# Gated attention with two MoE layers on one core: a shorter weight decode, two tiles in three terms, one chunk's decay a unit ahead, two chunks' outputs in two units

## The chip, the cores and the metric

The kernel runs on one core of one Trainium2 chip. The metric is device time in microseconds (us), the median of several executions of the same program; lower is better. The engines are TensorE (PE, matmuls; its weight loads are listed as PEld), VectorE (DVE), ScalarE (ACT), GpSimd (POOL) and SyncE (SP), whose queue issues nearly all DMAs. Each engine works through its own instructions strictly in program order and waits on semaphores of the others.

## The reference

What is computed, cut to its core (B=4, H=8, S=768, D=48; 3072 tokens, d_model 384, d_ff 2048):

```python
f = 1.0 / (1.0 + np.exp(-f_logit))
for t in range(S):
    state = f[:, :, t, :, None] * state + np.einsum('bhd,bhe->bhde', k[:, :, t], v[:, :, t])
    y[:, :, t] = np.einsum('bhd,bhde->bhe', q[:, :, t], state)
x = y.transpose(0, 2, 1, 3).reshape(B * S, H * D)
h = np.maximum(x @ w_in, 0.0)
x = h * h @ w_out                                      # MoE layer 0
h = x @ w_in2
x = np.where(h > 0, h, np.exp(np.minimum(h, 0)) - 1) @ w_out2   # MoE layer 1
```

The weights reach the chip as 64-bit floats. The kernel decodes them to 32-bit floats itself.

## The kernel before

**Units.** The 3072 tokens are six blocks of 512, and each layer has 16 tiles of 128 hidden columns. A unit u is one pair of block and tile. In unit u the kernel issues `up` of unit u (PE: the hidden values `ph`) and then `down` of unit u-2 (PE: the outputs `y`); `between` on ACT and DVE makes the operands `gg`, `gh`, `gl` of `down` from `ph`. Units 0 to 15 are block 0 of layer 0, units 16 to 31 block 1, and so on; units from 96 on are layer 1.

**Three terms and one term.** A value is split into a high and a low part (`hi`, `lo`, type fp32r), and a product is high x high + low x high + high x low, three matmuls of fp32r. In block 0 the tiles below `WHOLE` do it another way in `down`: one matmul in full f32 with the weights as decoded, which a DMA (`store_weights`, L411 and L413, on SP) copies into the weight tile; the second half of such a tile is split later, in block 1 (`split_rest`). Tiles from `WHOLE` on are split whole in block 0 (`split_up`, L434 on ACT for the high part and L435 on DVE for the low one).

**Decode.** In block 0 the decode of a weight tile is `begin` (two ACT instructions, L71 and L73) and, one unit later, `finish` (two DVE instructions, L81 and L82). L73 turns the top byte of a double's low word into its three highest bits and writes them as a 32-bit word over that low word; `finish` shifts, merges the three bits, and merges the sign. Layer 1 uses `decode`, which is not touched; it holds a DVE shift of the same shape (L59).

**Attention.** The sequence is 24 chunks g of 128 tokens (four batches x six). Chunks 0 to 3 and the first decodes are issued in START, an order written out by hand as a string of letters (f: load the forget logits `ff`; g: gate; d: decay scan on DVE; U: `up`; and so on). The later chunks are planned: `NEAR[g]` = a gives the unit in which chunk g meets its keys, and the other steps of the chunk stand at fixed distances from it. With d = a - 4 (g up to 12): load `ff` at d-2, load q and k and gate at d, decay at d+1, scale at d+2, load v at d+1. Steps planned for unit 1 or earlier are dropped by `at`; START has them. `f5` stands in START, and for chunk 5 (a = 8, d = 4) the plan loads `ff` once more in unit 2. The outputs of a chunk are `a_far` (PE L293, which adds the state, then a small ACT copy `seen`, L300), `a_out` (PE L308, ACT L316), `a_rows` (six small DMAs, L324) and `a_hi`, `a_lo` (the chunk's part of the block's `xh` and `xl`). For most chunks another chunk's `a_near` lies between `a_far` and `a_out` in the same unit; chunks 7 and 23, the last of their blocks, have none there. `plan` is issued ahead of a unit's matmuls, `behind` after them.

Of the kernel before, what the change touches and what calls it, by code (L numbers as in the profile page):

```python
# [11 lines left out]
F32 = mybir.dt.float32  # L12
F32R = mybir.dt.float32r
I32 = mybir.dt.int32
U32 = mybir.dt.uint32
U8 = mybir.dt.uint8
I64 = mybir.dt.int64
AF = mybir.ActivationFunctionType
ALU = mybir.AluOpType
PSUM = bass.MemoryType.PSUM  # L20

B, H, S, D = 4, 8, 768, 48
# [15 lines left out]
STAGED = 27  # L38
DIRECT = 3
EARLY = 14  # L40
WHOLE = 10
NEAR = dict(zip(range(B, NG), (5, 8, 10, 12, 19, 21, 23, 25, *range(28, 4 * NG - 23, 4))))
ORDER = np.r_[64:128, 63:-1:-1]
DMIN = 2.0**-52
# [21 lines left out]
def begin(nc, raw, out):  # L66

    words = raw.bitcast(U32).rearrange("p (n two) -> p n two", two=2)
    top = raw.bitcast(U8).rearrange("p (n b) -> p n b", b=8)[:, :, 3]
    hi, lo = words[:, :, 1], words[:, :, 0]  # L70
    nc.scalar.activation(out.bitcast(F32), hi.bitcast(F32), AF.Copy, scale=2.0**-112)  # L71

    nc.scalar.activation(lo, top, AF.Copy, scale=1 / 32, bias=-31 / 64)  # L73


def finish(nc, raw, out):

    words = raw.bitcast(U32).rearrange("p (n two) -> p n two", two=2)
    hi, lo = words[:, :, 1], words[:, :, 0]
    V = nc.vector  # L80
    V.scalar_tensor_tensor(out=out, in0=out, scalar=3, in1=lo, op0=ALU.logical_shift_left, op1=ALU.bitwise_or)  # L81
    V.scalar_tensor_tensor(out=out, in0=hi, scalar=0x80000000, in1=out, op0=ALU.bitwise_and, op1=ALU.bitwise_or)  # L82


def chunked(ctx, tc, ff, qk, vk, vz, wraw, mask, ident, flag, out):
# [6 lines left out]
    nc = tc.nc  # L92
    V, A, G, PE = nc.vector, nc.scalar, nc.gpsimd, nc.tensor

    one = ctx.enter_context(tc.tile_pool(name="one", bufs=1))
    two = ctx.enter_context(tc.tile_pool(name="two", bufs=2))
# [31 lines left out]
    def load_f(g):  # L128
        if g in (2, 3):
            if g == 2:  # L130
                st["f23"] = wpool.tile([ROWS, 2, 521], F32, tag="w", name="f23")
            t = st["f23"][:, g - 2]
        else:
            t = two.tile([ROWS, 521], F32, tag="ff", name=f"ff{g}")
        nc.sync.dma_start(out=t, in_=ff[g])
        st.setdefault(g, {})["ff"] = t

    def load_qk(g):
# [251 lines left out]
    def begin_weights(f):  # L390

        if f < EARLY:
            if f % 2 == 0:
                st["pair"] = wpool.tile([128, 2, 2 * DM], U32, tag="w", name=f"pair{f}")
            b = st["pair"][:, f % 2]
        else:
            b = two.tile([128, 2 * DM], U32, tag="dec", name=f"dec0_{f}")
        begin(nc, raws[0, f], b)
        decs[f] = b

    def finish_weights(f):
        finish(nc, raws.pop((0, f)), decs[f])

    def store_weights(f):

        wt[0, f] = t = wpool.tile([128, 2, 2, DM], F32R, tag="w", name=f"w0_{f}")
        if f >= WHOLE:
            return
# [6 lines left out]
    def split_up(f):  # L415
        b = decs.pop(f).bitcast(F32)
        if f < WHOLE:
            split(wt[0, f][:, :, 0:1], b[:, :DM])
# [13 lines left out]
    def split(t, b):  # L432
        hi, lo = (t[:, a].rearrange("r i m -> r (i m)") for a in range(2))
        A.activation(hi, b, AF.Copy)  # L434
        V.tensor_tensor(out=lo, in0=b, in1=hi, op=ALU.subtract)  # L435
# [11 lines left out]
    n1 = sum(layer == 0 for layer, _, _ in BLOCKS)  # L447
# [4 lines left out]
    def pieces(i, f):  # L452

        n = BLOCKS[i][2]
        return (slice(0, n // 2), slice(n // 2, n)) if (i, f) == final else (slice(0, n),)
# [21 lines left out]
    def between(i, f):  # L477
        layer, t0, n = BLOCKS[i]
        if i == 0 and f < WHOLE:

            r = one.tile([128, n], F32, tag="r", name=f"r{i}_{f}")
            gg = three.tile([128, n], F32, tag="gh", name=f"gg{i}_{f}")
            A.activation(r, hs[i, f][0], AF.Relu)
            A.activation(gg, r, AF.Square)
            hs[i, f] = (None, None, gg)
            return
        gh = three.tile([128, n], F32R, tag="gh", name=f"gh{i}_{f}")
        gl = three.tile([128, n], F32R, tag="gl", name=f"gl{i}_{f}")
        r = one.tile([128, n], F32, tag="r", name=f"r{i}_{f}")
        gg = two.tile([128, n], F32, tag="gg", name=f"gg{i}_{f}")  # L490
        if layer:
            t = two.tile([128, n], F32, tag="ff", name=f"t{i}_{f}")
        for c, ph in zip(pieces(i, f), hs[i, f]):
            if layer == 0:
                A.activation(r[:, c], ph, AF.Relu)  # L495
                A.activation(gg[:, c], r[:, c], AF.Square)

                if i == n1 - 1 or (i == 0 and f >= EARLY):
                    A.activation(gh[:, c], r[:, c], AF.Square)
                else:  # L500
                    V.tensor_tensor(out=gh[:, c], in0=r[:, c], in1=r[:, c], op=ALU.mult)  # L501
            else:
                A.activation(r[:, c], ph, AF.Relu, scale=-1.0)  # L503

                A.activation(t[:, c], r[:, c], AF.Tanh, scale=-0.5)  # L505
                A.activation(r[:, c], r[:, c], AF.Exp, scale=-1.0)  # L506
                V.scalar_tensor_tensor(out=t[:, c], in0=r[:, c], scalar=1.0, in1=t[:, c], op0=ALU.add, op1=ALU.mult)  # L507
                V.scalar_tensor_tensor(out=gg[:, c], in0=ph, scalar=0.0, in1=t[:, c], op0=ALU.max, op1=ALU.add)  # L508
                if (i, f) == final:
                    A.activation(gh[:, c], gg[:, c], AF.Copy)  # L510
                else:
                    V.tensor_copy(gh[:, c], gg[:, c])

            if (i, f) == final or i == 0:
                V.tensor_tensor(out=gl[:, c], in0=gg[:, c], in1=gh[:, c], op=ALU.subtract)
        hs[i, f] = (gh, gl, gg)
# [40 lines left out]
    plan, behind = {}, {}  # L557

    def at(slot, f, *args, to=plan):

        if slot > 1:
            to.setdefault(slot, []).append((f, args))
# [2 lines left out]
        at(f - 5, load_raw, 0, f)  # L565
    for g in range(B, NG):
        a = NEAR[g]
        d = a - (4 if g <= 3 * B else 6)
        at(d - 2, load_f, g)
        at(d, load_qk, g)  # L570
        at(d, a_gate, g)
        at(d + 1, a_decay, g)
        at(d + 2, a_scale, g)
        for h in (a_keys, a_transposed):
            at(a - (1 if g <= 3 * B else 2), h, g)
        at(d + 1 if g < B + 2 else max(d + 1, NEAR[g - 1] + 1), load_v, g)
        over = g > B and g != 2 * B
        if over:
            at(a, a_far, g - 1)
        at(a, a_near, g)  # L580
        if over:
            at(a, a_out, g - 1)
            at(a + 1, a_rows, g - 1)
        at(a, a_mask, g)
        at(a, a_states, g)
        if g in (2 * B - 1, NG - 1):
            for h in (a_far, a_out):
                at(a + 1, h, g)
            at(a + 2, a_rows, g)
            for h in (a_hi, a_lo):  # L590
                at(a + 3, h, g, to=behind)
        else:
            for h in (a_hi, a_lo):
                at(NEAR[g + 1] + 3, h, g)
# [6 lines left out]
    for f in range(NF):  # L601
        at(max(f - 3, 2 if f > 3 else 0), begin_weights, f)
        at(f - 2, finish_weights, f)
        if f < WHOLE:
            at(f + (NF - 2 if f < DIRECT else NF), split_rest, f)
# [10 lines left out]
    with tc.manual_schedule():  # L616
# [13 lines left out]
        for _ in range(3):  # L630
# [3 lines left out]
            "M": lambda: nc.sync.dma_start(out=msk, in_=mask),  # L634
            "T": lambda: [nc.sync.dma_start(out=tri[c:c + 64], in_=mask[c:c + 64, 64 - c:128 - c]) for c in (0, 64)],
            "f": load_f, "q": load_qk, "v": load_v, "r": lambda f: load_raw(0, f),
            "g": a_gate, "d": a_decay, "c": a_scale, "s": a_scores, "t": a_transposed, "m": a_mask, "k": a_state,
            "y": a_direct, "h": a_hi, "l": a_lo,
            "x": a_whole, "b": begin_weights, "w": finish_weights, "C": store_weights, "S": split_up, "W": busy,
            "U": lambda f: up(0, f), "B": lambda f: between(0, f),  # L640
            "L": lambda f: low(0, f),
        }
# [110 lines left out]
@with_exitstack  # L753
def gated_attention_moe(ctx: ExitStack, tc: tile.TileContext, ff, qk, vk, vz, nat, wraw, mask, ident, out):
    pool = ctx.enter_context(tc.tile_pool(name="flag", bufs=1))
    flag = pool.tile([1, 1], I32, name="flag")
    with ExitStack() as inner:
        chunked(inner, tc, ff, qk, vk, vz, wraw, mask, ident, flag, out)
    rv = tc.nc.values_load(flag[0:1, 0:1], min_val=0, max_val=1)
    with tc.If(rv == 1):  # L760
        with ExitStack() as inner:
            general(inner, tc, nat, wraw, ident, out)
# [58 lines left out]
```

## Time and profile before

| what | value |
|---|---|
| median of 3 runs | 885.45 us (886.34, 885.35, 885.45) |
| the profiled execution | 884.29 us |
| its span, first to last instruction | 882.2 us |
| PE busy | 867.3 us (98%) |
| DVE, ACT, POOL busy | 556.1, 454.2, 277.8 us |
| granted TensorE clock over the span | 0.998 |

The span is the part of the execution that the trace covers; 2.1 us of the profiled execution lie outside it. Matmuls are pipelined and their ends are modelled, so a busy PE can still be waiting: what counts is the distance from the start of one matmul to the start of the next. The profiled execution is 1.16 us shorter than the median of the three runs.

### The profile page before, as it was taken

What the parts mean: (1) busy time and instruction counts of PE and PEld (TensorE: products, weight loads), DVE (VectorE), ACT (ScalarE), POOL (GpSimd) and SP (SyncE); (2) the same over time, 40 slices, a digit from 0 to 9 for tenths busy, and PEclk for the clock granted to TensorE, in tenths of its full rate; (3) what the DMA queues carried; (4) which work ended last, traced back from release to release, by engine and by line L of the source; (5) the groups of instructions that cost most, each with busy time, mean ns of one, the idle gap of its engine ahead of it and who ended that gap; (6) DMA issues with size and microseconds to landing.
All of it is one profiled execution on the core that took longest, in us unless ns stands there. A gap on an engine that the chain in (4) does not pass through costs nothing.

```text
span 882.2 us, 16003 instructions
## 1 busy us (share of the span) xinstructions
PE 867.3 (98%) x6262; PEld 701.4 (80%) x6262; DVE 556.1 (63%) x841; ACT 454.2 (51%) x812; POOL 277.8 (31%) x248
## 2 busy tenths in 40 slices
PE   7999999999999999999999999999999999999996
PEld 4666788888888888888888888888888888888885
DVE  8989797876778777744331655655654664664543
ACT  5868745555445555454554544544444444444443
POOL 2011065423333333323232323233232332322331
PEclk9999999999999999999999999999999999999999
DMA  9993222235434434422676300100200100100001
GB/s 291 343 306 125 78 88 86 89 111 183 155 119 151 151 117 158 143 77 107 249 277 225 131 13 1 62 10 4 69 1 18 55 1 34 38 1 37 1 1 39
DMA packets 35779, 91.46 MB, mean 104 GB/s; under 512 B 5728, under 2 KB 12128, under 8 KB 35696
## 3 DMA queue, kind: packets, MB, share of 16 engines
q1 hardware_dynamic: 35552, 90.24, 30.6%
q8 instruction: 50, 0.82, 0.4%
q14 instruction: 33, 0.27, 0.1%
q10 hardware_dynamic: 144, 0.13, 0.0%
HBM read 64.78 MB, written 22.02 MB: 98 GB/s over the span
## 4 chain that ended last, share of the span: by engine, by line
PE 92%; DMA 4%; DVE 1%; SPq 1%; issue 0%; ACT 0%; DVEq 0%
PE y L538 44%; PE ph L474 44%; DMA raw<-wraw 2%; DMA q<-qk 1%; PE o L293 1%; PE o L308 1%; PE tp L209 1%; PE sk_a L232 1%; PE sk_a L241 1%; PE sk_h L241 0%; DVE ds L181 0%; PE sk_h L232 0%; DVE xl L355 0%; DVE pair L82 0%; DVE pair L81 0%
## 5 line engine op out<-in xcount | busy, mean ns | idle before, releaser
L521 POOL TENSOR_TENSOR gl<-gg,gh 128x512 fp32r<-128x512 f32 x175 | 234.2, 1338 | 451.8 <-PE ph L474 192.1
L538 PE MATMUL y<-gh,wf 128*128 128x512 f32 (+1 forms) x582 | 177.7, 387 | 0.0
L507 DVE SCALAR_TENSOR_TENSOR t<-r,t 128x512 f32<-128x512 f32 (+1 forms) x97 | 71.4, 736 | 154.8 <-ACT r L506 154.6
L538 PE MATMUL y<-gh,w 128*128 128x512 f32 x516 | 158.9, 389 | 0.0
L503 ACT ACTIVATE r<-ph 128x512 f32<-128x512 f32 (+1 forms) x97 | 57.8, 596 | 181.4 <-PE ph L474 176.5
L474 PE MATMUL ph<-xh,w 128*128 128x512 f32 x558 | 148.0, 400 | 0.3 <-DVE w L435 0.3
L474 PE MATMUL ph<-xh,wf 128*128 128x512 f32 (+1 forms) x582 | 146.4, 387 | 0.0
L538 PEld LDWEIGHTS y<-gh,wf 128*128 128x128 f32 x582 | 108.8, 188 | 22.2
L474 PEld LDWEIGHTS ph<-xh,wf 128*128 128x128 f32 x582 | 108.6, 188 | 22.3
L474 PEld LDWEIGHTS ph<-xh,w 128*128 128x128 f32 x558 | 101.4, 188 | 22.6 <-DVE w L435 0.9
L538 PEld LDWEIGHTS y<-gh,w 128*128 128x128 f32 x516 | 96.8, 188 | 20.2
L538 PE MATMUL y<-gl,wf 128*128 128x512 f32 (+1 forms) x291 | 112.5, 387 | 0.0
L495 ACT ACTIVATE r<-ph 128x512 f32<-128x512 f32 x86 | 51.3, 596 | 106.6 <-PE ph L474 89.2
L538 PE MATMUL y<-gl,w 128*128 128x512 f32 x258 | 100.4, 389 | 0.0
L474 PE MATMUL ph<-xl,wf 128*128 128x512 f32 (+1 forms) x291 | 81.0, 387 | 0.0
L474 PE MATMUL ph<-xl,w 128*128 128x512 f32 x279 | 78.5, 390 | 0.0
L501 DVE TENSOR_TENSOR gh<-r 128x512 fp32r<-128x512 f32 x68 | 46.8, 689 | 43.0 <-ACT r L495 43.0
L508 DVE SCALAR_TENSOR_TENSOR gg<-ph,t 128x512 f32<-128x512 f32 (+1 forms) x97 | 66.6, 686 | 10.4 <-DVE t L507 0.5
L538 PEld LDWEIGHTS y<-gl,wf 128*128 128x128 f32 x291 | 54.6, 188 | 11.2
L474 PEld LDWEIGHTS ph<-xl,wf 128*128 128x128 f32 x291 | 54.4, 188 | 11.1
L505 ACT ACTIVATE t<-r 128x512 f32<-128x512 f32 (+1 forms) x97 | 61.0, 629 | 3.1
L506 ACT ACTIVATE r<-r 128x512 f32<-128x512 f32 (+1 forms) x97 | 61.0, 628 | 3.1
(112 smaller groups left out, 1026.6 us busy)
## 6 DMA issues: line engine op xcount, KB each, us to landing
raw<-wraw SPq DMA_DIRECT2D x32, 768.0 KB, 7.1
wst<-w SPq DMA_DIRECT2D x16, 768.0 KB, 3.3
wf<-wst SPq DMA_DIRECT2D x16, 768.0 KB, 4.7
ff<-ff SPq DMA_DIRECT2D x23, 227.9 KB, 7.0
k<-qk SPq DMA_DIRECT2D x22, 224.0 KB, 3.4
q<-qk SPq DMA_DIRECT2D x22, 224.0 KB, 4.4
x2d<-yo SPq DMA_DIRECT2D x18, 256.0 KB, 2.8
x<-x2d SPq DMA_DIRECT2D x18, 256.0 KB, 3.2
```

The source lines that it names most:

```text
L209: PE.transpose(tp[:, p, 0:ROWS], k[:, p], idt[:ROWS, :ROWS])
L232: PE.matmul(sc[j][64 * c:64 * c + 64, p], k[lo:hi, p, 64 * c:64 * c + 64], q[lo:hi, p, 64 - 64 * c:128 - 64 * c], start=True, stop=True,)
L474: PE.matmul(ph, w[:, a, 0, 128 * k:128 * k + 128], b[:, k, c], start=(m == 0), stop=(m == len(todo) - 1))
L495: A.activation(r[:, c], ph, AF.Relu)
L501: V.tensor_tensor(out=gh[:, c], in0=r[:, c], in1=r[:, c], op=ALU.mult)
L503: A.activation(r[:, c], ph, AF.Relu, scale=-1.0)
L505: A.activation(t[:, c], r[:, c], AF.Tanh, scale=-0.5)
L506: A.activation(r[:, c], r[:, c], AF.Exp, scale=-1.0)
L507: V.scalar_tensor_tensor(out=t[:, c], in0=r[:, c], scalar=1.0, in1=t[:, c], op0=ALU.add, op1=ALU.mult)
L508: V.scalar_tensor_tensor(out=gg[:, c], in0=ph, scalar=0.0, in1=t[:, c], op0=ALU.max, op1=ALU.add)
L521: G.tensor_tensor(out=gl, in0=gg, in1=gh, op=ALU.subtract)
L538: PE.matmul(yp_[i][m][:, c], w[:, 128 * m:128 * m + 128], b[:, c], start=(f == 0 and n_ == 0), stop=(f == NF - 1 and n_ == len(terms) - 1) ...
```

## The change

Five edits. (1) `begin` writes the three bits as a byte into the lowest byte of the high word, and `finish` becomes a plain shift and one step that takes the sign and the three bits from the high word. (2) `WHOLE` goes from 10 to 8, so tiles 8 and 9 of block 0 are split whole and use three terms; their `gh` is a square on ACT. (3) For chunk 5 d is a - 5, so its gate, decay, scale and loads stand one unit earlier, and the second load of `ff` falls out of the plan. (4) For chunks 7 and 23 `a_out` stands one unit after `a_far`, and `a_rows` follows behind that unit's matmuls. (5) The first load of forget logits is two DMAs, of 260 and 261 columns.

```diff
-WHOLE = 10
+WHOLE = 8
...
 def begin(nc, raw, out):
...
-    nc.scalar.activation(lo, top, AF.Copy, scale=1 / 32, bias=-31 / 64)
+    nc.scalar.activation(octets[:, :, 4], octets[:, :, 3], AF.Copy, scale=1 / 32, bias=-31 / 64)
...
 def finish(nc, raw, out):
...
-    V.scalar_tensor_tensor(out=out, in0=out, scalar=3, in1=lo, op0=ALU.logical_shift_left, op1=ALU.bitwise_or)
-    V.scalar_tensor_tensor(out=out, in0=hi, scalar=0x80000000, in1=out, op0=ALU.bitwise_and, op1=ALU.bitwise_or)
+    V.tensor_scalar(out=out, in0=out, scalar1=3, scalar2=None, op0=ALU.logical_shift_left)
+    V.scalar_tensor_tensor(out=out, in0=hi, scalar=0x80000007, in1=out, op0=ALU.bitwise_and, op1=ALU.bitwise_or)
...
-        nc.sync.dma_start(out=t, in_=ff[g])
+        for c in (slice(0, 260), slice(260, 521)) if g == 0 else (slice(0, 521),):
+            nc.sync.dma_start(out=t[:, c], in_=ff[g, :, c])
...
-                if i == n1 - 1 or (i == 0 and f >= EARLY):
+                if i == n1 - 1 or (i == 0 and f not in range(10, EARLY)):
...
-        d = a - (4 if g <= 3 * B else 6)
+        d = a - (5 if g == B + 1 else 4 if g <= 3 * B else 6)
...
         if g in (2 * B - 1, NG - 1):
-            for h in (a_far, a_out):
-                at(a + 1, h, g)
-            at(a + 2, a_rows, g)
+            at(a + 1, a_far, g)
+            at(a + 2, a_out, g)
+            at(a + 2, a_rows, g, to=behind)
```

On DVE, in units 5 and 6 of block 0, these rows stood one behind the other before; `ds_91<-ff_453` is chunk 5's decay, `w_6` the low half of weight tile 6, `raw_7` the decode of tile 7, and `k_516`, `q_515` chunk 5's keys and queries.

```order
L259 COPY_PREDICATED sd_95<-tri,sk_h 128x256
L247 TENSOR_TENSOR s_97<-state_99,wc_447 112x192
L248 TENSOR_TENSOR s_98<-sk_a_550,s_97 112x192
L250 TENSOR_TENSOR state_99<-sk_h,s_98 112x192
L179 MEMSET lim 112x9
L181 SCALAR_TENSOR_TENSOR ds_91<-ff_453,lim 112x520
L182 RECIPROCAL lim<-ds_91 112x8
L183 SCALAR_TENSOR_TENSOR ds_91<-ff_453,lim 112x521
L192 TENSOR_TENSOR ends<-ends 112x8
L435 TENSOR_TENSOR w_6_599<-pair_486,w_6_599 128x384
L81 SCALAR_TENSOR_TENSOR pair_486<-pair_486,raw_7_441 128x768
```

With the change the same place on DVE reads so, from the last row of the decay on (line numbers are one lower).

```order
L191 TENSOR_TENSOR ends<-ends 112x8
L434 TENSOR_TENSOR w_5_532<-pair_454,w_5_532 128x384
L79 TENSOR_SCALAR pair_491<-pair_491 128x768
L80 SCALAR_TENSOR_TENSOR pair_491<-raw_6_428,pair_491 128x768
L258 COPY_PREDICATED sd_95<-tri,sk_a_559 128x256
L258 COPY_PREDICATED sd_95<-tri,sk_h 128x256
L246 TENSOR_TENSOR s_97<-state_99,wc_448 112x192
L247 TENSOR_TENSOR s_98<-sk_a_559,s_97 112x192
L249 TENSOR_TENSOR state_99<-sk_h,s_98 112x192
L202 TENSOR_TENSOR k_480<-k_480,ds_91 112x512
L202 TENSOR_TENSOR q_479<-q_479,ds_91 112x512
L434 TENSOR_TENSOR w_6_600<-pair_491,w_6_600 128x384
```

The decay has moved up by one unit, ahead of `w_5` and the decode of tile 6; behind the state now come chunk 5's keys and queries, and then `w_6`.

On PE, at units 13 and 14 of block 0, chunk 7's two passes (`o`) stood together ahead of `up` of tile 13 before. Each pass is a run of small matmuls on the two halves o_0 and o_1; the first two rows of a run are shown and dots stand for the rest.

```order
L538 MATMUL y_2_468<-gl_10_977,w_10_846 128x512
L293 MATMUL o_0_1156<-q_790,s_97 48x64 x2
L293 MATMUL o_1_1157<-q_790,s_98 48x64 x2
...
L308 MATMUL o_0_1156<-sd_96,vk_1001 48x64
L308 MATMUL o_1_1157<-sd_96,vk_1001 48x64
...
L474 MATMUL ph_13_0_1205<-xh_405,w_13_1113 128x512 x6
L474 MATMUL ph_13_0_1205<-xl_406,w_13_1113 128x512 x3
```

With the change PE meets them so.

```order
L537 MATMUL y_2_467<-gl_10_988,w_10_847 128x512
L292 MATMUL o_0_1173<-q_788,s_97 48x64 x2
L292 MATMUL o_1_1174<-q_788,s_98 48x64 x2
...
L473 MATMUL ph_13_0_1201<-xh_406,w_13_1130 128x512 x6
L473 MATMUL ph_13_0_1201<-xl_407,w_13_1130 128x512 x3
...
L537 MATMUL y_2_467<-gl_11_1042,w_11_961 128x512
L307 MATMUL o_0_1173<-sd_96,vk_1012 48x64
L307 MATMUL o_1_1174<-sd_96,vk_1012 48x64
...
L473 MATMUL ph_14_0_1254<-xh_406,w_14_1196 128x512 x6
```

The second pass has moved behind `up` of tile 13 and `down` of tile 11, so a whole unit of matmuls now lies between the two passes. The same happens to chunk 23 at units 73 and 74.

## Rows read from the trace of the kernel before

**Rows 1.** The page: busy time by engine, share of the span, instructions.

```profile
PE 867.3 (98%) x6262; PEld 701.4 (80%) x6262; DVE 556.1 (63%) x841; ACT 454.2 (51%) x812; POOL 277.8 (31%) x248
```

**Rows 2.** Windows: start:end, length (us); busy us of PE, PEld, DVE, ACT, POOL; clock, DMA share, GB/s.

```profile
35.00:45.00 10.00, 10.00 (x36) 6.02 (x35) 8.77 (x14) 9.62 (x16) 0.99 (x2) 1.00 1.03 354
65.00:75.00 10.00, 10.00 (x109) 6.71 (x102) 9.38 (x17) 8.73 (x16) 1.40 (x3) 1.00 0.69 217
```

**Rows 3.** Timeline of START: start us, length us, instruction, idle before and its releaser.

```profile
0.75 0.41 SPq L135 DMA_DIRECT2D ff<-ff  x1
...
3.66 0.42 ACT L169 ACTIVATE ff<-ff 112x260 f32<-112x260 f32 x1 [1.64 <-DMA ff<-ff]
...
4.57 1.47 DVE L181 TENSOR_TENSOR_SCAN ds<-ff,lim 112x260 f32<-112x260 f32 x2 [2.04 <-ACT ff L170]
...
6.96 0.64 ACT L169 ACTIVATE ff<-ff 112x521 f32<-112x521 f32 x1 [1.66 <-DMA ff<-ff]
...
27.68 7.99 PE L463 MATMUL ph<-x,pair 128*128 128x512 f32 x18 [0.22 <-ACT x L342]
```

**Rows 4.** Chain in order of time, units 10, 13, 14: start us, us, what.

```profile
80.20 2.57 PE y L538 x6
...
96.44 2.29 PE ph L474 x9
...
100.78 2.04 PE ph L474 x9
```

**Rows 5.** Timeline of PE, units 2 and 3, then units 5 and 6.

```profile
35.51 2.74 PE L538 MATMUL y<-gg,w 128*128 128x512 f32 x6
...
40.16 2.74 PE L538 MATMUL y<-gg,w 128*128 128x512 f32 x6
...
51.14 2.74 PE L538 MATMUL y<-gg,w 128*128 128x512 f32 x6
...
54.37 1.45 PE L474 MATMUL ph<-xh,w 128*128 128x512 f32 x5 [0.26 <-DVE w L435]
...
56.34 1.02 PE L538 MATMUL y<-gg,w 128*128 128x512 f32 x2
```

**Rows 6.** Timeline of DVE, unit 6: the low half of weight tile 6.

```profile
53.76 0.56 DVE L435 TENSOR_TENSOR w<-pair,w 128x384 fp32r<-128x384 f32 x1
```

**Rows 7.** Timeline of PE: passes of chunk 6, chunk 7 and chunk 23.

```profile
87.75 0.66 PE L293 MATMUL o<-q,s 48*48 48x64 f32 x32
88.24 0.22 PE L232 MATMUL sk_a<-q,k 48*64 48x64 f32 x1
...
94.04 0.66 PE L293 MATMUL o<-q,s 48*48 48x64 f32 x32
95.72 0.72 PE L308 MATMUL o<-sd,vk 64*48 64x64 f32 x32 [1.02 <-ACT seen L300]
...
383.50 0.72 PE L308 MATMUL o<-sd,vk 64*48 64x64 f32 x32 [0.26 <-ACT seen L300]
```

**Rows 8.** Three instructions by line: ns min/median/max, first and last start us.

```profile
L59 DVE TENSOR_SCALAR dec<-dec x16: 560/1326/1478, 174.5 to 450.6; 128x768 uint32<-128x768 uint32 x16
...
L81 DVE SCALAR_TENSOR_TENSOR pair<-pair,raw x14: 945/951/972, 25.4 to 85.9; 128x768 uint32<-128x768 uint32 x14
...
L73 ACT ACTIVATE raw<-raw x16: 892/912/958, 19.5 to 93.0; 128x768 uint32<-128x768 uint8 x16
```

**Rows 9.** Timelines: low half of weight tile 4 on DVE, `up` of tile 4 on PE.

```profile
41.60 0.55 DVE L435 TENSOR_TENSOR w<-pair,w 128x384 fp32r<-128x384 f32 x1
...
43.05 1.18 PE L474 MATMUL ph<-xh,w 128*128 128x512 f32 x4
```

**Rows 10.** Timelines of SP, ACT and PE: chunk 7 on its way into block 1.

```profile
97.93 3.83 SPq L324 DMA_DIRECT2D x<-x  x6
...
107.30 0.51 ACT L349 ACTIVATE xh<-x 128x384 fp32r<-128x384 f32 x1
...
108.83 1.52 PE L474 MATMUL ph<-xh,w 128*128 128x512 f32 x6
```

More of the change, by code (lines that the diff above doesn't have):

```diff
@@ L68, in begin @@
     words = raw.bitcast(U32).rearrange("p (n two) -> p n two", two=2)
-    top = raw.bitcast(U8).rearrange("p (n b) -> p n b", b=8)[:, :, 3]
-    hi, lo = words[:, :, 1], words[:, :, 0]
-    nc.scalar.activation(out.bitcast(F32), hi.bitcast(F32), AF.Copy, scale=2.0**-112)
-    nc.scalar.activation(lo, top, AF.Copy, scale=1 / 32, bias=-31 / 64)
+    octets = raw.bitcast(U8).rearrange("p (n b) -> p n b", b=8)
+    nc.scalar.activation(out.bitcast(F32), words[:, :, 1].bitcast(F32), AF.Copy, scale=2.0**-112)
+    nc.scalar.activation(octets[:, :, 4], octets[:, :, 3], AF.Copy, scale=1 / 32, bias=-31 / 64)
 def finish(nc, raw, out):
-    words = raw.bitcast(U32).rearrange("p (n two) -> p n two", two=2)
-    hi, lo = words[:, :, 1], words[:, :, 0]
+    hi = raw.bitcast(U32).rearrange("p (n two) -> p n two", two=2)[:, :, 1]
     V = nc.vector
-    V.scalar_tensor_tensor(out=out, in0=out, scalar=3, in1=lo, op0=ALU.logical_shift_left, op1=ALU.bitwise_or)
-    V.scalar_tensor_tensor(out=out, in0=hi, scalar=0x80000000, in1=out, op0=ALU.bitwise_and, op1=ALU.bitwise_or)
+    V.tensor_scalar(out=out, in0=out, scalar1=3, scalar2=None, op0=ALU.logical_shift_left)
+    V.scalar_tensor_tensor(out=out, in0=hi, scalar=0x80000007, in1=out, op0=ALU.bitwise_and, op1=ALU.bitwise_or)
 def chunked(ctx, tc, ff, qk, vk, vz, wraw, mask, ident, flag, out):
```

## The prediction

> **What bounds the kernel now.** I read the busy shares first, then the clock, then the timeline of PE by the distance from one matmul's start to the next. PE is busy 98% of the span [rows 1], at full clock: the granted clock is 1.00 in the windows that I read [rows 2], which is the 2.4 GHz level. From the first `ph` at 27.68 [rows 3] to the end its starts follow each other at the bare pace of the matmuls, so a change pays only if it makes START shorter, takes passes off PE, or removes one of the few places where PE waits. I find three: weight tile 6 [rows 5], chunk 7 and chunk 23 [rows 7]. The other engines only have to deliver in time. They are not far from late: DVE works 9.38 of 10 us and ACT 8.73 between 65 and 75 us, and ACT 9.62 of 10 between 35 and 45 [rows 2].
>
> **Tiles 8 and 9 in three terms.** A `down` in f32 is six passes and takes 2.57 us; nine fp32r matmuls of the same shape take 2.04 [rows 4]. Two tiles make 2 x (2.57 - 2.04) = 1.06 us less on PE, and nothing hides PE. What it adds (a whole split in place of half, a square on ACT, a subtraction on DVE per tile) is paid on ACT and DVE two units before `down` needs it, and DVE gets more back from the decode (below). In block 1 two half splits fall away.
>
> **Chunk 5 a unit earlier.** From one f32 `y` to the next, a unit with no attention work takes 40.16 - 35.51 = 4.65 us; unit 6 takes 56.34 - 51.14 = 5.20 [rows 5]. The 0.55 us between them is a wait: the second matmul of `ph`, the first to use the low half of `w_6`, starts at 54.37, and DVE made that half from 53.76 to 54.32 [rows 5, 6], because chunk 5's decay stood ahead of it in DVE's queue. The change puts the decay ahead of `w_5` instead and chunk 5's two scalings of keys and queries ahead of `w_6`. The scalings are shorter than the decay, their loads move up too and are no longer queued behind a weight load, and DVE had been idle in the unit before. What is late next is `w_5`: the decay now precedes it, but that unit has the slack which DVE spent idle. I take the whole 0.55; the bounds are 0 and 0.55. The gate (one tanh on ACT, one POOL operation) moves with it: ACT pays 0.64 us, the length of such a tanh [rows 3], ahead of `w_4`. The low half of `w_4` ends at 42.15 and PE starts that `ph` at 43.05 and needs the low half one matmul later, 0.23 later by nine in 2.04 [rows 4, 9]: 1.13 us of slack. It loses 0.3 (START, below) and 0.64, and keeps about 0.2 at worst. The dropped second load of chunk 5's `ff` takes one DMA off SP's queue and moves no PE time by itself.
>
> **Chunk 7's outputs in two units.** The second pass starts 95.72 - 94.04 = 1.68 us after the first; where other work follows a first pass at once, as at chunk 6, it starts 88.24 - 87.75 = 0.49 later [rows 7]. PE waits 1.19 us for the small ACT copy `seen`. With a unit between the passes the copy has over 4 us, and the wait goes. The price is a second seam: the `ph` behind an attention pass takes 2.29 in place of 2.04 [rows 4], 0.25 us, and I add 0.09 for the step from `y` to the pass, an estimate of less than half a matmul. Net 1.19 - 0.34 = 0.85. At chunk 23 the trace shows only 0.26 of wait [rows 7], about what the new seam costs: 0. The six row copies, 3.83 us of SP's queue before [rows 10], and the loads queued behind them start about one unit later against PE. Then the chunk's `xh`, which ACT made at 107.30 to 107.81 for a `ph` at 108.83 [rows 10], could be late: the copies were issued from 97.93 to 101.76, so they had been issued 5.5 us before ACT used them, and they move by one unit, about 4.1 us (18 matmuls by the pace above). 1.4 us is left for the last of them to land.
>
> **The shorter decode.** `finish` was two DVE instructions of 0.95 us each [rows 8]. The first becomes a plain shift. Layer 1 already has a shift of this shape: 0.56 at its shortest, 1.33 in the middle and 1.48 at its longest [rows 8]. The long ones lie in stretches where POOL subtracts `gl` all the time; in block 0 DVE does that, and POOL is busy only 0.99 and 1.40 of 10 us [rows 2]. I take 0.56, so 0.39 us less DVE per tile, about 6 us over 16 tiles; the other end is 1.48, 0.53 more. For PE this is worth nothing now, since the only `w` that came late is `w_6`; it pays for what the other edits add to DVE. The Trainium skill, page "SBUF — State Buffer", section "Who interferes with whom", has a rule against such a shift: a DVE instruction in a two-port mode and a GpSimd instruction that uses SBUF lock each other out for a whole instruction. By that rule the shift is short where POOL rests and waits out a POOL instruction where it does not; the sum above stands if POOL rests, and rival 2 is the other case. On ACT the second instruction now writes bytes, 8 bytes apart, in place of words. No row shows a byte store. The word store takes 0.91 [rows 8]; reading bytes there costs nothing that can be seen, so I take 0.91 again, with twice that as the other end (rival 3).
>
> **The first load in two halves.** DVE's START is one dense queue that begins when ACT has the first forget tile: issue at 0.75, first tanh at 3.66, first scan at 4.57 [rows 3], and it ends in `ph` at 27.68. ACT already works in halves, so half the bytes are enough to begin. 2.9 us pass from the issue to the tanh, most of it a fixed delay; what can fall away is half of the transfer. An estimate: the tile is 112 x 521 x 4 = 233 KB, at the 354 GB/s that the DMA engines reach when full [rows 2] 0.66 us, and half of it 0.33. I take 0.3, since short rows do not move faster. The ends: 0.5 gained, if the lone first transfer runs below that rate, and 0.1 lost, if all later loads are pushed back by the extra issue of 0.41 and one of them becomes the late one. The second half is not needed until half a scan, 0.74 us, later. The Trainium skill, page "DMA: Bandwidth & Descriptors", section "Rules for kernel authors", advises against splitting, since both parts go through the same engines one after the other. By it the first half still lands first, but nothing else does; it is rival 4.
>
> **The sum.** 1.06 + 0.55 + 0.85 + 0.3 = 2.76 us. The profiled execution of 884.29 would become 881.53. It lay 1.16 below the median of the runs, so against the median of 885.45 the forecast is 882.7 us.
>
> **Rivals.**
> 1. *The gain is partly taken back at a deadline.* PE reaches every unit of block 0 up to 2.8 us earlier, and ACT, which gains nothing from the decode, may not: at `w_4` (slack 0.2 at worst) or at block 1's first unit (1.4). A miss would cost about 1 us. For it: ACT's 9.62 of 10. Against it: ACT was waiting for DVE's decode just ahead of the high half of `w_4`, and that decode gets shorter. 883.9 us.
> 2. *The shift runs in its long form.* At 1.33 each decode costs DVE 0.38 more instead of 0.39 less. Between 65 and 75 us DVE has 0.62 us free [rows 2] and would get two decodes (0.76), a subtraction and half a split more, some 1.5 us; PE would wait about 1 us in each 10 of the 30 us around there. Against it: POOL's small share. 885.7 us.
> 3. *The byte store is slow: the other side.* The place is ACT between 27 and 45 us. Four such stores stand ahead of `w_4` from the third decode on. Each may take 0.05 us more at worst, and 0.28 at best, before PE waits at `ph` of tile 4; doubled they put 3.6 us there, less the 0.2 to 1.1 of slack, and from there ACT, at 8.73 plus 2 x 0.91 of 10 us [rows 2], stays full and loses about 3 more. It decides against the change when the waits pass 2.76 us, which is about 0.8 us more per store. At double, 882.7 + 3 + 3 = 888 us at most, about 887.
> 4. *START does not get shorter*, because later loads, not DVE, set it. For it: the DMA engines can be full, as their share of 1.03 between 35 and 45 us shows [rows 2]. Against it: DVE is never idle between the first scan and the last mask. 883.0 us.
>
> **Chances.** The forecast as it stands 0.60; rival 4, 0.12; rival 1, 0.13; rival 2, 0.06; rival 3, 0.06; another place where the change does nothing, 0.03. A measurement of this kernel can tell about 0.2%, 1.77 us. Forecast and rival 4 are both past that (885.45 - 883.0 = 2.4), but a smaller START or half of one term would bring a few of them inside: faster 0.75 with a part of rival 1. Same 0.17: most of rival 1, half of rival 2, the last case. Slower 0.08. The range takes in 0.8 us of further gain (START's 0.5 and a positive chunk 23, with the run-to-run spread) and reaches up past rival 1: 881.4 to 884.8.
>
> **What would show it.** In the changed profile: `y` of tiles 8 and 9 as nine records in 2.04; unit 6 from `y` to `y` in 4.65; no releaser `seen` ahead of L307 in block 0, and two `ph` of 2.29 where one was; the shift at 0.56 in all 16; the byte store at 0.91; first `ph` at 27.4. Wrong would be: a PE wait at `ph` of tile 4 or 5 for DVE's low half, or at block 1's first `ph` for `xh`; a first `ph` at 27.7 or later; byte stores over 1.2 us.

## The result: 0.67% slower, and the profile after

| | before | changed |
|---|---|---|
| median of 6 runs | 885.40 us | 891.52 us (891.06 to 892.38) |
| ratio to before, 95% interval | | 1.0067, 1.0054 to 1.0080 |
| span of the profiled execution | 882.2 us | 890.6 us |
| last matmul of `y` ends at | 874.50 | 882.71 |

The forecast was 882.7 us and faster; the time came out 6 us above the kernel before and outside the range. Busy time by engine in the changed kernel answers to [rows 1]: PE has hardly changed, DVE has 5 us less, ACT 19 us more.

```profile
PE 869.8 (98%) x6268; PEld 703.7 (79%) x6268; DVE 550.9 (62%) x841; ACT 472.8 (53%) x812; POOL 275.9 (31%) x248
```

The instructions of the decode, by line (least, median and longest duration in ns, first and last start), answer to [rows 8]. L72 is the byte store, L79 the plain shift.

```profile
L72 ACT ACTIVATE raw<-raw x16: 1902/1954/1975, 19.5 to 100.5; 128x768 uint8<-128x768 uint8 x16
...
L79 DVE TENSOR_SCALAR pair<-pair x14: 539/554/562, 24.7 to 93.0; 128x768 uint32<-128x768 uint32 x14
```

The byte store takes 1.95 us where the word store took 0.91: 16 x 1.04 = 17 us more on ACT, all within the 80 us of block 0. The shift is short, as forecast. What that does to PE is in the list of PE's waits between 27 and 110 us (who waits for whom, us in total, times, longest). Before, the only waits there were the ones in [rows 3], [rows 5] and [rows 7].

```profile
PE o L307 <- ACT seen L299: 3.6, 2, 1.8
PE ph L473 <- ACT r L482: 1.5, 1, 1.5
PE ph L462 <- ACT r L482: 1.4, 1, 1.4
PE ph L473 <- ACT w L433: 0.9, 1, 0.9
```

None of these waits is for the stored bytes themselves. They are for whatever stands behind the decode in ACT's queue: the relu of a tile, a high half, the small copy `seen`. The timelines of ACT and of PE at chunk 6 show one of them: the store begins at 92.90, the relu, the square and `seen` follow it, and PE, done with the first pass and the states, starts the second pass at 96.19.

```profile
92.90 1.96 ACT L72 ACTIVATE raw<-raw 128x768 uint8<-128x768 uint8 x1
94.61 0.67 ACT L494 ACTIVATE r<-ph 128x512 f32<-128x512 f32 x1
95.31 0.63 ACT L495 ACTIVATE gg<-r 128x512 f32<-128x512 f32 x1
95.97 0.23 ACT L299 ACTIVATE seen<-o 48x4 f32<-48x4 f32 x2
...
96.19 0.98 PE L307 MATMUL o<-sd,vk 64*48 64x64 f32 x32 [1.75 <-ACT seen L299]
97.10 1.22 PE L473 MATMUL ph<-xh,w 128*128 128x512 f32 x2
```

Behind this wait the clock falls too. The windows have length, busy us of PE, PEld, DVE, ACT and POOL, then the granted clock, the DMA share and GB/s: PE was busy 0.44 of 2 us, and the two stretches that follow are granted 0.62 and 0.53, which is near the lower of the two levels, 1.2 GHz. Five matmuls of `ph` there, from 97.69 on, take 0.43 us from start to start in place of 0.23.

```profile
94.00:96.00 2.00, 0.44 (x32) 0.32 (x22) 1.22 (x2) 1.94 (x4) 0.00 (x0) 1.00 0.03 8
96.00:98.00 2.00, 1.81 (x34) 1.57 (x35) 1.83 (x6) 0.96 (x4) 0.00 (x0) 0.62 0.00 0
98.00:100.00 2.00, 2.00 (x6) 1.52 (x6) 0.82 (x3) 1.95 (x4) 0.00 (x0) 0.53 0.02 5
```

START, which answers to [rows 3], did get shorter at its beginning: first tanh at 2.87 in place of 3.66, first scan at 3.77 in place of 4.57, first `ph` at 27.03 in place of 27.68. But already at the third tile PE waits for the relu of an earlier one.

```profile
2.87 0.42 ACT L168 ACTIVATE ff<-ff 112x260 f32<-112x260 f32 x1 [0.84 <-DMA ff<-ff]
...
3.77 1.47 DVE L180 TENSOR_TENSOR_SCAN ds<-ff,lim 112x260 f32<-112x260 f32 x2 [1.24 <-ACT ff L169]
...
27.03 5.42 PE L462 MATMUL ph<-x,pair 128*128 128x512 f32 x12 [0.24 <-ACT x L341]
33.84 2.84 PE L462 MATMUL ph<-x,pair 128*128 128x512 f32 x6 [1.39 <-ACT r L482]
```

### The profile page after: what moved, and what is told of

Same layout as the page of the kernel before. It is cut to its first block, busy times and chain, and to the rows that moved or that the text cites. A ratio compares the mean times of both kernels' runs of the same rounds, so it can differ in the third digit from the quotient of the medians.

```text
span 890.6 us, 16009 instructions
## 1 busy us (share of the span) xinstructions
PE 869.8 (98%) x6268; PEld 703.7 (79%) x6268; DVE 550.9 (62%) x841; ACT 472.8 (53%) x812; POOL 275.9 (31%) x248
## 4 chain that ended last, share of the span: by engine, by line
PE 90%; ACT 3%; DMA 1%; issue 1%; DVE 0%; SPq 0%; ACTq 0%; DVEq 0%
PE ph L473 43%; PE y L537 42%; PE o L307 1%; PE o L292 1%; PE tp L208 1%; PE sk_a L231 1%; DMA vk<-vk 1%; ACT raw L72 1%; PE sk_a L240 0%; PE sk_h L240 0%; ACT w L433 0%; SPq L323 0%; ACT pair L70 0%; ACT x L315 0%; PE sk_h L231 0%
## 5 line engine op out<-in xcount | busy, mean ns | idle before, releaser
L537 PE MATMUL y<-gh,w 128*128 128x512 f32 x528 | 162.6, 389 | 0.0
L537 PEld LDWEIGHTS y<-gh,w 128*128 128x128 f32 x528 | 99.1, 188 | 20.6
L537 PE MATMUL y<-gl,w 128*128 128x512 f32 x264 | 102.7, 389 | 0.0
```

The source lines that it names most:

```text
L537: PE.matmul(yp_[i][m][:, c], w[:, 128 * m:128 * m + 128], b[:, c], start=(f == 0 and n_ == 0), stop=(f == NF - 1 and n_ == len(terms) - 1) ...
```

## The experiments

The theory after the result: the byte store alone carries the loss, through ACT's time; the other four edits bring roughly what the sum gave them. The rivals: the edits that move work earlier have waits of their own; the new decode hurts only together with the extra squares of tiles 8 and 9; byte stores slow what runs beside them. Twelve kernels were run. For reading them side by side, this table has the start (us) of PE's `ph` at some tiles of block 0, and the end of the last matmul, each from the timeline of that kernel's profile.

| kernel | tile 0 | 3 | 4 | 5 | 7 | 10 | 12 | 13 | 15 | end |
|---|---|---|---|---|---|---|---|---|---|---|
| before | 27.68 | 37.68 | 43.05 | 48.97 | 59.23 | 77.86 | 89.72 | 96.36 | 104.70 | 874.50 |
| changed | 27.03 | 39.04 | 45.57 | 53.55 | 63.25 | 84.03 | 97.10 | 103.28 | 112.47 | 882.71 |
| changed, word store | 26.89 | 38.11 | 43.47 | 49.38 | 59.09 | 77.75 | 89.43 | 94.33 | 103.52 | 873.76 |
| the same, stored twice | 27.05 | 39.16 | 45.41 | 53.02 | 62.75 | 83.18 | 95.70 | 100.64 | 109.83 | 880.08 |
| word store, fourth tile first | 27.27 | 37.28 | 42.65 | 48.56 | 58.27 | 76.93 | 88.63 | 93.53 | 102.72 | 872.97 |

**1. The changed kernel with the word store.** `begin` and `finish` are those of before, all else is the change.

```diff
-    nc.scalar.activation(octets[:, :, 4], octets[:, :, 3], AF.Copy, scale=1 / 32, bias=-31 / 64)
+    nc.scalar.activation(lo, top, AF.Copy, scale=1 / 32, bias=-31 / 64)
...
-    V.tensor_scalar(out=out, in0=out, scalar1=3, scalar2=None, op0=ALU.logical_shift_left)
-    V.scalar_tensor_tensor(out=out, in0=hi, scalar=0x80000007, in1=out, op0=ALU.bitwise_and, op1=ALU.bitwise_or)
+    V.scalar_tensor_tensor(out=out, in0=out, scalar=3, in1=lo, op0=ALU.logical_shift_left, op1=ALU.bitwise_or)
+    V.scalar_tensor_tensor(out=out, in0=hi, scalar=0x80000000, in1=out, op0=ALU.bitwise_and, op1=ALU.bitwise_or)
```

> The changed kernel with the decode of before: ACT stores a word (0.92 us), DVE two instructions of 0.95. Theory: the byte store of 1.95 us on ACT is the whole loss, the other four edits bring what the prediction gave them. Then 885.45 - 2.76 = 882.7 us, or 882.3 with the 0.65 that the first ph of the changed kernel came earlier (27.03 in place of 27.68), and no PE wait over 0.3 us between the third unit and chunk 7. Rival: the edits that move work earlier (START, chunk 5's gate ahead of w_4) have waits of their own at w_4 or w_5; then 884 to 885.5 us, with a PE wait at the ph of tile 4 or 5 left in the trace.

Measured: 883.62 us against 885.90 for before, measured beside it, ratio 0.9975 (0.9966 to 0.9984): 2.3 us faster than before, and between the theory's 882.7 and the rival's 884. The table splits the distance to the changed kernel: of 8.95 us at the end, 0.93 arise ahead of tile 3, 1.17 at tile 4, 2.07 at tile 5, 2.11 at tile 10, 1.39 at tile 12, 1.28 at tile 13 (where the clock fell). Against before, the table shows 1.17 us less from tile 3 to the end (835.65 in place of 836.82); the rest of the 2.3 us would have to lie in START, and these two profiles do not show it, since tile 3 starts 0.43 later here. No wait is left at tiles 4 and 5. Those that are left, between 27 and 110 us:

```profile
PE ph L464 <- ACT r L484: 0.6, 1, 0.6
PE ph L475 <- DVE w L436: 0.3, 1, 0.3
PE ph L464 <- ACT x L343: 0.2, 1, 0.2
```

The second is at tile 11, the first in START, where no theory had put a wait. The waits at `w_4` and `w_5` that the rival asked for do not exist.

**2. The new decode alone, in the kernel before.** Of the change's diff only the lines in `begin` and `finish` are there.

> The kernel before with the new decode alone (byte store on ACT, plain shift on DVE). Theory: it carries the whole loss, which is 6.07 + 2.76 = 8.8 us, so 894 us, with 1.95 for the store and PE waits at the ph of tiles 3 to 5 and at the far-to-out steps of chunks 5 and 6. Rival: the new decode hurts only together with the other edits (the extra square on ACT in tiles 8 and 9, the gate ahead of w_4); then at most half of it, 886 to 889 us.

Measured: 894.61 us, ratio 1.0096 (1.0081 to 1.0112), 8.7 us slower than before. The loss needs none of the other edits.

**3. A 16-bit store in place of the byte.**

```diff
...
+    halves = raw.bitcast(U16).rearrange("p (n h) -> p n h", h=4)
...
-    nc.scalar.activation(octets[:, :, 4], octets[:, :, 3], AF.Copy, scale=1 / 32, bias=-31 / 64)
+    nc.scalar.activation(halves[:, :, 2], octets[:, :, 3], AF.Copy, scale=1 / 32, bias=-31 / 64)
```

> The changed kernel, but ACT stores the low bits as a 16-bit number into the low half of the high word in place of a byte; the DVE instructions are those of the changed kernel. If only a store of single bytes is slow: 0.92 us for the store and 882.3 us, or some tenths less than the kernel with the word store, since DVE keeps its shorter decode. If every store narrower than a word is slow: 1.95 us for the store and 891.5 us, as the changed kernel. Something between, 1.4 us, would give about 886 us.

Measured: 892.16 us, ratio 1.0065 (1.0051 to 1.0078), and the store as slow as that of a byte:

```profile
L74 ACT ACTIVATE raw<-raw x16: 1912/1949/1976, 19.8 to 100.3; 128x768 uint16<-128x768 uint8 x16
```

**4. The forms by themselves.** Copies of 128x768 behind the last output of the kernel before, on a scratch tile; nothing reads them.

```diff
+            A.activation(o32[:, :, 1], i8[:, :, 3], AF.Copy, scale=1 / 32, bias=-31 / 64)
+            A.activation(o8[:, :, 4], i8[:, :, 3], AF.Copy, scale=1 / 32, bias=-31 / 64)
+            A.activation(flat8, i8[:, :, 3], AF.Copy, scale=1 / 32, bias=-31 / 64)
+            A.activation(flat8, pr.bitcast(U8)[:, 0:2 * DM], AF.Copy, scale=1 / 32, bias=-31 / 64)
+            A.activation(o8[:, :, 4], view(pr, U32, 2)[:, :, 1].bitcast(F32), AF.Copy, scale=1 / 32, bias=-31 / 64)
+            A.activation(po.bitcast(F32)[:, 0:2 * DM], i8[:, :, 3], AF.Copy, scale=1 / 32, bias=-31 / 64)
+            V.tensor_copy(o8[:, :, 4], i8[:, :, 3])
+            V.tensor_copy(o32[:, :, 1], i8[:, :, 3])
```

> The kernel before, with a group of copies of 128x768 added behind the last output, twice over: on ACT byte in, word out, 8 bytes apart; byte in, byte out, 8 bytes apart; byte in 8 bytes apart, bytes out side by side; bytes side by side in and out; word in, byte out 8 bytes apart; byte in, words out side by side; and on DVE the first two forms. Only the durations are of interest; the added time at the end is not. If the width of the output sets the price, every byte output on ACT takes 1.95 and the word outputs 0.92. If it is the step of 8 bytes between single bytes, bytes side by side take 0.92. If it is byte in together with byte out, the form with a word in takes 0.92.

The groups by line, ACT and then DVE; L669 to L676 are the eight copies in the order of the diff (busy us, mean ns of one, idle before).

```profile
L673 ACT ACTIVATE probe_out<-probe 128x768 uint8<-128x768 f32 x2 | 3.8, 1900 | 0.1
L670 ACT ACTIVATE probe_out<-probe 128x768 uint8<-128x768 uint8 x2 | 3.8, 1900 | 0.1
L674 ACT ACTIVATE probe_out<-probe 128x768 f32<-128x768 uint8 x2 | 1.8, 890 | 0.1
L671 ACT ACTIVATE probe_out<-probe 128x768 uint8<-128x768 uint8 x2 | 1.8, 878 | 0.1
L669 ACT ACTIVATE probe_out<-probe 128x768 uint32<-128x768 uint8 x2 | 1.8, 876 | 4.7 <-DVE probe_out L663 2.9 <-DVE probe_out L676 1.7
L672 ACT ACTIVATE probe_out<-probe 128x768 uint8<-128x768 uint8 x2 | 1.7, 842 | 0.1
...
L675 DVE COPY probe_out<-probe 128x768 uint8<-128x768 uint8 x2 | 2.0, 1018 | 15.1 <-ACT probe_out L674 15.1
L676 DVE CAST probe_out<-probe 128x768 uint32<-128x768 uint8 x2 | 1.1, 560 | 0.1
```

On ACT neither the byte as such nor the step of 8 bytes is slow. Bytes side by side take 0.84 to 0.88 us, words 8 bytes apart 0.88, and what is read makes no difference (L670 against L673). Only single bytes 8 bytes apart take 1.90, and by experiment 3 single half-words too. DVE has two prices as well, 1.02 for bytes 8 bytes apart and 0.56 for words. Other steps were not measured, nor half-words side by side, and why the narrow stores are slow stays open.

**5. Dose: the word store twice, on experiment 1.**

```diff
     nc.scalar.activation(lo, top, AF.Copy, scale=1 / 32, bias=-31 / 64)
+    nc.scalar.activation(lo, top, AF.Copy, scale=1 / 32, bias=-31 / 64)
```

> The changed kernel with the word store, done twice in a row into the same place, so that ACT pays some 0.85 us more per tile without any byte store. Theory: the changed kernel lost through ACT's time alone (1.03 per tile, 7.9 us between it and the kernel with the word store); then some 5.5 to 6.5 us come back here, 889 to 890 us, with the same PE waits at the ph of tiles 3 to 5. Rival: byte stores also slow what runs beside them, and the time of ACT is the smaller part: under 887 us.

Measured: 889.87 us, ratio 1.0048 (1.0034 to 1.0061), 6.25 us above experiment 1 (6.32 in the table). Its waits are those of the changed kernel:

```profile
PE o L310 <- ACT seen L302: 2.9, 2, 1.5
PE ph L465 <- ACT r L485: 1.5, 1, 1.5
PE ph L476 <- ACT r L485: 1.1, 1, 1.1
...
PE ph L476 <- ACT w L436: 0.7, 1, 0.7
```

So ACT's time is the cause, and the rival that byte stores slow their neighbours (under 887) falls. Of the 7.9 us between experiment 1 and the changed kernel 1.65 are missing here. Most of that is the clock: it stayed up here, and tile 13 adds 0.04 us; in the changed kernel it adds 1.28.

**6. Each other edit undone, on experiment 1.** Four kernels: one load for the first forget tile; ten f32 tiles; chunk 5 back where it was; both output passes in one unit.

```diff
-        for c in (slice(0, 260), slice(260, 521)) if g == 0 else (slice(0, 521),):
-            nc.sync.dma_start(out=t[:, c], in_=ff[g, :, c])
+        nc.sync.dma_start(out=t, in_=ff[g])
```

```diff
-WHOLE = 8
+WHOLE = 10
...
-                if i == n1 - 1 or (i == 0 and f not in range(10, EARLY)):
+                if i == n1 - 1 or (i == 0 and f >= EARLY):
```

```diff
-        d = a - (5 if g == B + 1 else 4 if g <= 3 * B else 6)
+        d = a - (4 if g <= 3 * B else 6)
```

```diff
-            at(a + 1, a_far, g)
-            at(a + 2, a_out, g)
-            at(a + 2, a_rows, g, to=behind)
+            for h in (a_far, a_out):
+                at(a + 1, h, g)
+            at(a + 2, a_rows, g)
```

> The changed kernel with the word store (883.62 us), and the first forget tile in one load again. Theory: START ends when the fourth raw weight tile has landed, not when DVE is done; the split lets DVE begin 0.65 to 0.79 us earlier, but the landing (30.5 to 30.7 in the three profiles with the split, 29.55, 31.0 and 32.3 in three without) is set by how fast the loads follow each other. Then the first ph comes near 27.7 again and the time moves by 0.2 us at most on the mean, 883.4 to 884.0. Rival: the split is worth its 0.3 or more, since loads issued on a landing follow earlier: 884.0 to 884.6. Rival: the split costs, by one more issue of 0.41 in the load queue: 883.2.

> The changed kernel with the word store, and weight tiles 8 and 9 in f32 again. By the prediction's term: 1.06 more, 884.7 us. Rival: the two splits on ACT and DVE that three terms need made the second ph matmul of tile 11 wait 0.48 us and the out pass of chunk 6 wait 0.19; these go with the undoing, so only 0.4 more, 884.0 us.

> The changed kernel with the word store, and chunk 5's gate, decay and loads where they were. By the prediction's term: 0.55 more, 884.2 us, with PE waiting for the low half of tile 6 near 54 us. Rival: the wait belongs to a queue that has moved meanwhile and does not come back: 883.6 us.

> The changed kernel with the word store, and both output passes of chunks 7 and 23 in one unit again. By the prediction's term: 0.85 more for chunk 7, nothing for chunk 23, 884.5 us, and a wait of 1.2 us for the ACT copy in front of the second pass of chunk 7. Besides: a PE wait of 0.40 us for an ACT copy among the last matmuls is in each of the three profiles with the split outputs and in none of the three without; if it hangs on chunk 23's edit it goes here and the time is 884.1 us; if it hangs on the arrival time alone it stays.

| undone | median, us | ratio to before (95%) | what PE's timeline shows, beside START |
|---|---|---|---|
| split first load | 884.46 | 0.9986 (0.9977 to 0.9995) | nothing |
| tiles 8, 9 in three terms | 883.78 | 0.9979 (0.9970 to 0.9988) | +0.53, then -0.34 |
| chunk 5 earlier | 884.19 | 0.9984 (0.9975 to 0.9993) | +0.70 at tile 7 |
| outputs in two units | 885.46 | 0.9997 (0.9988 to 1.0006) | +0.99 at the passes, +0.38 behind them, +0.10 at chunk 23 |

Before had 885.59 beside these four, and experiment 1 had a ratio of 0.9975. Chunk 5 and chunk 7 came as the theory said: the two waits are back, the second at `seen` for 1.0 us. PE's waits with chunk 5 undone (the first row) and with the outputs undone:

```profile
PE ph L475 <- DVE w L436: 0.8, 2, 0.4
...
PE o L309 <- ACT seen L301: 1.0, 1, 1.0
```

One of the two waits in the first row is that of tile 11, which experiment 1 has too. With the outputs undone the median moved by 1.8 us, more than the 0.85 that the theory gave; 1.47 of it lie behind START by the table.

The intervals are 1.6 us wide, so the medians alone tell only the last kernel from experiment 1; the sizes are from the traces. The three-term tiles went as the rival said: the step of tile 8 gives its 0.53, but that of tile 9 costs 0.34 net, because the added `gh`, `gl` and split on ACT and DVE make tile 11's low half and chunk 6's second pass late (experiment 7 tells tile 9 from tile 8).

The first load's theory was about START. Its median did not come as forecast: 884.46 lies in the range of the rival that gives the split its 0.3 or more, though not clear of experiment 1 by the intervals. The trace bears the mechanism out: the first `ph` is back at 28.05, and tile 3 starts at 38.60, 0.49 later than in experiment 1, because the fourth raw tile landed 0.48 later (31.15 against 30.67). Over all profiles that landing is no earlier with the split than without (below), so whether the split had a part in it is not shown. The decode of the fourth raw tile (`raw_3`) stands in ACT's queue ahead of the relu of tile 0, and PE cannot begin tile 2 without that relu. Rows of ACT and PE in experiment 1:

```profile
30.69 0.90 ACT L71 ACTIVATE pair<-raw 128x768 f32<-128x768 f32 x1 [2.02 <-DMA raw<-wraw]
...
32.91 2.84 PE L464 MATMUL ph<-x,pair 128*128 128x512 f32 x6 [0.60 <-ACT r L484]
...
38.11 1.95 PE L475 MATMUL ph<-xh,w 128*128 128x512 f32 x6
```

From that decode to `ph` of tile 3 it is 7.42 us here, 7.43, 7.40, 7.41 and 7.41 in the four undone kernels and 7.43 in experiment 4: where a word is stored once and ACT waits for the load, its landing sets the end of START. In the eleven profiles whose load order is that of before but for the split first load, it landed at 30.49 to 32.09 with the split (seven) and at 29.55 to 32.30 without (four). In the profile of before it was 29.55, the earliest of all, and START had 0.7 us to spare (8.11 from decode to tile 3).

**7. The fourth tile's load ahead of chunk 4's.**

```diff
-x0 r2 k1 m1 s2 d3 f4 q4 t2 y1 c3 b0 k2 s3 m2 x1 r3 t3 b1 ...
+x0 r2 k1 m1 s2 d3 r3 f4 q4 t2 y1 c3 b0 k2 s3 m2 x1 t3 b1 ...
```

Three kernels have this move: experiment 1; experiment 1 with tile 9 in f32 besides, by the set below in place of the comparisons with `WHOLE`; and the kernel before.

```diff
+FULL = {*range(WHOLE), 9}
...
-        if i == 0 and f < WHOLE:
+        if i == 0 and f in FULL:
```

> The changed kernel with the word store, and in START the load of the fourth raw tile issued ahead of the three loads of chunk 4's forget tile, keys and queries in place of behind them. Theory: in five profiles PE's unit behind START begins 7.42 to 7.45 us after that tile has landed, and three loads of some 0.87 stand ahead of it; so it lands near 28, START's other work binds (first ph 26.89 plus 10.0) and that unit begins near 36.9 in place of 38.1 to 38.6: 1.2 us or more off, 2.3 + 1.2 = 3.5 us below the kernel before. Rival: the next raw tile, which lands 1.9 us after, or chunk 4's loads bind at once in its place: 0 to 0.4 us gained, 2.3 to 2.7 below the kernel before.

> The kernel of the run above (fourth raw tile first), and tile 9 in f32 again, tile 8 alone in three terms. With both tiles undone the traces showed the step of tile 8 0.53 longer and that of tile 9 0.34 shorter, since waits at tile 11's low half (0.48) and at chunk 6's second pass (0.19) went away. If the work for tile 9 alone makes these waits: 0.3 us below the run above. If the work for tile 8 makes them, or both: up to 0.5 us above it.

> The kernel before with the one move in START alone: the fourth raw tile's load ahead of chunk 4's three. Its profile has that tile at 29.55, two others with the same START at 31.0 and 32.3, and from about 29.3 on every late us is a us of PE. Theory: the median falls by 0.9 to 1.5 us and the spread of the runs (2 us) shrinks. Rival: DVE's dense queue binds START in most executions, as the prediction had it: no change.

Measured, against 886.03 for before: 882.23 us, ratio 0.9962 (0.9949 to 0.9975) with the word store; 882.20, the same ratio, with tile 9 in f32 besides; 885.01, ratio 0.9994 (0.9985 to 1.0003) for the move alone in the kernel before. In the first of them ACT no longer waits, and PE goes from tile 0 to tile 3 without a pause:

```profile
28.95 0.92 ACT L71 ACTIVATE pair<-raw 128x768 f32<-128x768 f32 x1
...
27.27 7.99 PE L464 MATMUL ph<-x,pair 128*128 128x512 f32 x18 [0.22 <-ACT x L343]
37.28 1.95 PE L475 MATMUL ph<-xh,w 128*128 128x512 f32 x6
```

The first two of the three beat both before and the change: they are 3.8 us below before, and before was 6 below the change. Tile 9 in f32 shows its 0.3 to 0.4 us in the trace (tile 12 comes 11.32 us after tile 10, in place of 11.70) and not in the medians. The move alone is inconclusive: its profile has the tile in time and the same START as the profile of before, as it should, but the median's fall of 1.0 us is not clear of noise, and its runs still spread over 2 us. The rival, no change, is not excluded for before. What else spreads the runs of before was not found.

## Why the prediction was wrong, step by step

**The byte store: the step that failed.** "No row shows a byte store. [...] so I take 0.91 again, with twice that as the other end." It takes 1.95, a little over the other end; over 1.2 was one of the prediction's own signs of being wrong. The value was taken from the word store of the same shape, on the ground that reading bytes cost nothing; but reading and writing bytes are not alike (experiment 4). Of the two ends the wrong one was chosen for the sum, and rival 3, which had the store right, was given 0.06.

**Rival 3 was itself too small**, 887 where 891.5 came. It counted the high half of tile 4 and a full ACT queue behind it. It did not name what else stands in that queue ahead of PE: the relu at tile 2 (1.4) and at tile 5 (1.5), `seen` twice (3.6). It also left out the clock, about 1.2 us (1.28 at tile 13, against 0.04 in experiment 5). And it was summed on 882.7, while the kernel with the word store takes 883.62 and START with a slow store begins tile 3 8.53 us after the fourth decode, not 7.42. Two sums among the rivals do not come out either: 882.7 + 3 + 3 is 888.7 and not 888, and 882.7 with a miss of about 1 us is 883.7 and not rival 1's 883.9.

**The shift: right.** 0.54 to 0.56 in all 16; rival 2 falls. What it is worth to PE is not shown, since no run joins the short shift to a fast store. The Trainium skill, page "SBUF — State Buffer", section "Who interferes with whom", has the instruction that comes second wait for the whole of the first. In this trace POOL is the one that waits: its copy of 8 numbers per partition, 0.20 us when alone, took 1.26 beside a split and a shift of DVE and ended at 82.63, 0.05 after the shift (POOL and DVE timelines of the changed kernel). The two other copies that lie beside a shift end 0.05 after it too, at 41.10 and 51.63. The order fits less well: the copy below began 0.66 us ahead of the shift and still ended behind it. The profile's spans on POOL are rough, so who has to wait is not settled here.

```profile
81.37 1.26 POOL L192 COPY ends<-ds 112x8 f32<-112x8 f32 x1 [1.43 <-DVE ends L191]
...
82.03 0.55 DVE L79 TENSOR_SCALAR pair<-pair 128x768 uint32<-128x768 uint32 x1
```

**Tiles 8 and 9: mechanism right, size wrong.** Each `down` is 0.53 us shorter, as summed. "Paid on ACT and DVE two units before `down` needs it, and DVE gets more back from the decode" was the weak part: with the decode of before DVE gets nothing back, and 0.19 of 1.06 is left. In the changed kernel the short shift does free DVE, but ACT is late; whether DVE's time would have paid for tile 9 beside a fast store is not shown.

**Chunk 5: right.** Between tiles 3 and 7 experiment 1 is 0.57 us shorter than before, for 0.55; undone, it costs 0.70. No wait at `w_4` came of it. **Chunk 7: right, a little small**, 0.99 undone for 0.85, and 0.38 more from a wait at the tile behind. **Chunk 23:** 0.10 for nothing.

**START: the first `ph` moved more than the term, and it was worth less.** The term was 0.3, its upper bound 0.5; in the changed profile the first tanh came 0.79 earlier and the first `ph` 0.65. The tanh is as early in all nine profiles with the split (2.83 to 2.94, against 3.65 to 3.91 in the five without), but the first `ph` is not: 26.89 to 28.70 against 27.66 to 28.74. "DVE's START is one dense queue" fits the profile of before, but DVE is not what START ends with elsewhere. In six of the seven profiles with a single word store and the load order of before, the fourth raw tile is, and then an earlier first `ph` buys nothing. This was rival 4's cause. The Trainium skill's advice against splitting (page "DMA: Bandwidth & Descriptors", section "Rules for kernel authors", whose row is on two halves by partitions; here the columns were split) fits the stream as a whole, which did not get faster: the fourth tile landed at 30.49 at the earliest with the split, at 29.55 without. The first half alone did land 0.8 us earlier (2.84 against 3.64 for the whole). With the fourth tile's load moved, both profiles with the split have their first `ph` 0.4 to 0.7 earlier than the one of the kernel before with the same move (27.27 and 27.00 against 27.66), and tile 3 as well (37.28 and 37.04 against 37.66).

**The base of the sum.** That the profiled execution lay 1.16 below the median was noted and then only carried over. Part of it has a cause that the traces show: of the eleven profiles with that load order it is the one in which the fourth raw tile landed first. In the profile of experiment 4, which has the same START, it landed 1.46 us later and tile 3 began 0.78 later. The rest stays open, since the kernel before with that load moved still spreads over 2 us. A sum on a favourable execution can hide the bound that holds in others.

**The total of the other four edits** came near the sum, 2.3 us of 2.76, but partly by luck. Behind START the terms add up to 2.46 and the traces show 1.17, after a wait of 0.4 us in the last unit (below) that the sum did not have. The other 1.1 would have to come from START, whose term was 0.3; that is inferred from the medians and not seen in a trace.

## What to carry to other kernels

When one edit rests on an instruction form that no row shows, the chances have to turn on that form, above all when its instruction stands in an in-order queue ahead of things PE waits for: what counts is everything behind it, not its own result. Of the byte stores measured here the one with its elements side by side was cheap, and the one with its elements 8 bytes apart cost twice as much; the duration of such a form can be taken from a short probe beforehand. And before a queue of loads is taken for hidden, its last landing should be looked up against the first instruction that needs it, in more than one execution.

## What was not expected

Half-words and bytes stored 8 bytes apart cost ACT 1.90 to 1.95 us for 768 per partition, words at the same step 0.88, bytes side by side 0.84 to 0.88. DVE: 1.02 for bytes 8 bytes apart, 0.56 for words.

In the last unit a wait of 0.4 us on PE for an ACT copy (at 881.22 in the changed kernel) stands in every profile with at least three of the four other edits, and in none of before or of the kernels made from it by one edit. Ahead of it a DVE instruction of 0.43 us takes 1.30, while POOL, which began 0.29 earlier, subtracts; in the profile of before the two start together, DVE takes its 0.43 and POOL 1.58 in place of 1.31. DVE and POOL in experiment 1:

```profile
867.12 1.30 DVE L508 SCALAR_TENSOR_TENSOR t<-r,t 128x256 f32<-128x256 f32 x1 [0.46 <-ACT r L507]
...
866.83 1.31 POOL L522 TENSOR_TENSOR gl<-gg,gh 128x512 fp32r<-128x512 f32 x1 [2.78 <-DVE gh L513]
```

Undoing any one edit leaves it, so which of them decides who comes first stays open.
